# Sums of the first pair's operands made by GpSimd during the sequence stage and kept in DRAM

## The chip, the core and the metric

The kernel runs on one core of one Trainium2 chip. The metric is the device time of one execution in microseconds (us); lower is better. Five engines work side by side, each with an instruction queue that runs in order: TensorE (PE in the profile; its weight loads are PEld), VectorE (DVE), ScalarE (ACT), GpSimd (POOL) and SyncE (SP), which here only issues DMA transfers. ACT issues some transfers as well. An instruction that waits for a semaphore holds up everything behind it on its engine.

## The reference

Two branches work on x (2048 x 640, fp32) and are mixed by a gate for each row. Cut to what matters:

```python
g = sigmoid((x * gate_w).sum(-1, keepdims=True))
# A: Fourier mixing
a = einsum("bsd,ed->bse", x, dft_hid_re);  b = einsum("bsd,ed->bse", x, dft_hid_im)
y = einsum("ts,bse->bte", dft_seq_re, a) - einsum("ts,bse->bte", dft_seq_im, b)
# B: product-key experts, 32 heads, 16 x 16 keys, two best of 256 experts for each head
q = einsum("nd,dhc->nhc", x, w_q);  s1, s2 = scores of the halves of q with k1, k2
top_s, top_e = the two best sums of the two best of s1 and of s2
act = gelu(einsum("nd,nhkd->nhk", x, u[top_e]))
out = einsum("nhk,nhk,nhkd->nd", softmax(top_s), act, v[top_e])
return g * y + (1 - g) * out
```

## The kernel before

All large products are made in three fp32r matmuls (`mm3`, lines 127 to 129): each operand is split into a high half, a copy on ACT (line 122), and a low half, a subtraction on GpSimd or DVE (line 123).

**The sequence stage.** The sequence transform is done first, on x. It runs over 128 *pieces*, numbered n: w (real, imaginary) x c (four column blocks of 512 output rows) x s (16 blocks of x). For each piece SP loads a 128 x 512 tile `wf` of the DFT matrix five pieces ahead (`load_piece`, line 158), it is split three pieces ahead into the ring `WS` (`split_piece`; the low half on GpSimd), and PE makes 15 matmuls with it into five banks. After 16 pieces the five banks are copied to the staging tiles `ST` (line 212, ACT), gated by g on DVE (`gate_piece`, line 191) and stored to the DRAM tiles `pd[w, c]` (`store_piece`, line 198, ACT's queue). One such group is called a block q = 4w + c, and there are five `ST` tiles of 128 x 512, so a block is stored before the next is copied.

**What runs beside it.** From piece 31 to 70 the scores of branch B are made, then until the end of the stage the *experts*: DVE builds one-hot tiles `hot` (lines 539 to 541, three operations a tile, two tiles a set), PE multiplies them (line 563, 16 small matmuls a set, into a bank), and DVE sums the bank into `cd` (lines 547 and 549), which SP stores to the DRAM tile `gd` (line 553). Sets go in twos until the last pieces: six one-hot operations and four operations of sums a round. They are put between the matmuls by a pump with credits (`run_bg`), so their place on each engine is fixed when the program is written. Near the end of the stage DVE also makes sums of the hidden DFT matrices (`make_sums`, lines 648 to 652, tiles `tf` and `ts`), whose splits go to ACT, GpSimd and DVE.

**The last part.** The hidden transform is applied to what lies in `pd`, for two *pairs* b = 0 and 1 of column blocks, by a scheme with seven products in place of eight: `UNITS = ("a11", "a12", "s1", "s2", "s4", "s3", "a22")`. a11, a12, a21 and a22 are the blocks `pd[col - 1, 2 * b + row - 1]` (the first index of `pd` is real or imaginary), and s1, s2, s4 and s3 are sums of them: s1 = a22 + a21, s3 = a21 + a11, s2 = s1 + a11, s4 = s2 + a12. A unit has five steps k, 35 steps a pair. Step m multiplies the split operand (`step`); five steps ahead `split_step` splits it, out of raw tiles `ra` which `load_a` has loaded (line 705) and, for the s units, `add_a` has summed (line 708, DVE). In pair 0 and in pair 1 alike, the tile "s" holds s1, then s2, then s4: it is loaded with a22, and a21, a11 and a12 are added to it in turn, so that a11 and a12 are loaded twice. Raw tiles come from a free list of 19 (`take`, `give`). The experts' result enters by a product with v: `load_z` loads its parts, `split_z` multiplies them on DVE (lines 749 to 753) and splits them into `zo`, and `z_group` multiplies. At the end of a unit the banks are emptied by `post` (DVE and ACT) and, after a12, by a copy on ACT on line 860 into `ST[:, 4]`.

**What sets the order.** Every helper is hung on a place with `at(n, f, ...)`: it is called after piece n, or after step m as place 128 + m, in the order in which the `at` lines stand. Each engine's queue then runs its own instructions in that order.

## Time and profile before

| | |
|---|---|
| median of 3 runs | 794.71 us (794.21 to 794.85) |
| the profiled execution | 794.76 us, its span 793.0 us |
| PE busy | 778.2 us, 98% of the span, 4167 matmuls |
| DVE busy | 549.0 us, 69% |
| ACT, POOL busy | 275.1 us (35%), 338.7 us (43%) |
| mean granted TensorE clock | 0.996 |
| moved | 119.55 MB, 151 GB/s |

In the profile the engines stand by the names above; L123 is line 123 of the kernel before, and a name like `ra<-pd` is what an instruction writes and reads. Matmuls are pipelined, so that the recorded durations overlap: the pace of PE is read from start to start. An engine's idle time is told with what ended it.

### The profile page before, as it was taken

Reading aid. Unit: us, or ns where it says so; the run is one execution under the profiler, and the core shown is the slowest. Engines: PE = TensorE matmul, PEld = TensorE weight load, DVE = VectorE, ACT = ScalarE, POOL = GpSimd, SP = SyncE. Lnnn points to the kernel's source line nnn. Section 1 sums busy time; section 2 is a strip of 40 time slices with the busy share of each in tenths; the row PEclk is TensorE's granted clock in tenths of the full one; section 3 lists DMA queues with packets and bytes.
Section 4 is the critical chain, followed back from the end, with each engine's and each line's share of the span. In section 5 each row is a group of like instructions: output and inputs, shape, how many; then the busy total and the mean of one; then the engine's idle time right before and its main releaser. Section 6 shows DMA issues by size and latency. Waiting matters only on the chain.

```text
span 793.0 us, 10954 instructions
## 1 busy us (share of the span) xinstructions
PE 778.2 (98%) x4167; PEld 626.0 (79%) x4167; DVE 549.0 (69%) x658; ACT 275.1 (35%) x444; POOL 338.7 (43%) x234
## 2 busy tenths in 40 slices
PE   9999999999999999999999999999999997999997
PEld 6677677888888888888888888887887875888886
DVE  5851021286888799499969589989999938518651
ACT  3434223322315322532353551311333522534350
POOL 5432224315234241533415693334355453558270
PEclk9999999999999999999999999999999998999999
DMA  9876895503022330205213533235434586675321
GB/s 341 315 292 191 283 340 190 196 0 113 14 100 69 124 113 14 99 14 181 80 60 120 196 119 98 76 112 154 139 132 155 167 291 235 216 218 196 129 82 66
DMA packets 62787, 119.55 MB, mean 151 GB/s; under 512 B 8848, under 2 KB 15888, under 8 KB 62480
## 3 DMA queue, kind: packets, MB, share of 16 engines
q1 hardware_dynamic: 49984, 101.42, 38.3%
q10 hardware_dynamic: 12752, 17.45, 6.2%
q8 instruction: 32, 0.52, 0.3%
q14 instruction: 19, 0.16, 0.1%
HBM read 98.91 MB, written 19.93 MB: 150 GB/s over the span
## 4 chain that ended last, share of the span: by engine, by line
PE 90%; DVE 5%; DMA 3%; issue 1%; SPq 1%; ACT 0%; DVEq 0%; ACTq 0%
PE b L127 29%; PE b L129 28%; PE b L128 28%; PE b L299 2%; DMA xr<-in_xn 1%; PE b L563 1%; DMA wf<-in_wsre 1%; DMA ra<-pd 1%; PE b L311 1%; DVE tmp L547 0%; DVE hot L541 0%; DVE tf L651 0%; DVE tf L650 0%; DVE ST L191 0%; DVE ts L123 0%
## 5 line engine op out<-in xcount | busy, mean ns | idle before, releaser
L123 POOL TENSOR_TENSOR WS<-wf,WS 128x512 fp32r<-128x512 f32 x128 | 190.5, 1494 | 279.4 <-ACT WS L122 267.5
L127 PE MATMUL b<-WS,X 128*128 128x512 f32 x640 | 254.6, 398 | 1.2 <-ACT X L122 1.2
L129 PE MATMUL b<-WS,X 128*128 128x512 f32 x640 | 249.8, 390 | 0.5 <-DVE X L123 0.4
L128 PE MATMUL b<-WS,X 128*128 128x512 f32 x640 | 249.7, 390 | 0.3 <-POOL WS L123 0.3
L127 PEld LDWEIGHTS b<-WS,X 128*128 128x128 f32 x640 | 120.3, 188 | 34.6 <-issue 8.1
L129 PEld LDWEIGHTS b<-WS,X 128*128 128x128 f32 x640 | 120.1, 188 | 26.9 <-DVE X L123 1.3
L128 PEld LDWEIGHTS b<-WS,X 128*128 128x128 f32 x640 | 120.3, 188 | 24.2 <-POOL WS L123 0.7
L122 ACT ACTIVATE WS<-wf 128x512 fp32r<-128x512 f32 x128 | 80.2, 628 | 131.1 <-PE b L129 82.1
L413 DVE TENSOR_REDUCE mm<-sc 128x64 f32<-128x1024 f32 x32 | 39.0, 1219 | 45.0 <-ACT sc L399 44.5
L123 POOL TENSOR_TENSOR xl<-xf,xh 128x640 fp32r<-128x640 f32 x16 | 33.0, 2086 | 72.7 <-ACT xh L122 72.7
L127 PE MATMUL b<-WU,xh 128*128 128x512 f32 x160 | 62.7, 392 | 0.0
L129 PE MATMUL b<-WU,xl 128*128 128x512 f32 x160 | 62.3, 389 | 0.0
L128 PE MATMUL b<-WU,xh 128*128 128x512 f32 x160 | 62.3, 389 | 0.0
L399 ACT ACTIVATE sc<-b 128x512 f32<-128x512 f32 x32 | 20.5, 641 | 113.9 <-PE b L129 113.9
L123 POOL TENSOR_TENSOR WS<-ra,WS 128x512 fp32r<-128x512 f32 x32 | 45.2, 1434 | 28.5 <-ACT WS L122 28.5
L708 DVE TENSOR_TENSOR ra<-ra 128x512 f32<-128x512 f32 x40 | 37.6, 986 | 15.3 <-DMA ra<-pd 11.7
L314 DVE TENSOR_TENSOR WU<-b,WU 128x512 fp32r<-128x512 f32 (+1 forms) x16 | 7.8, 490 | 56.5 <-ACT WU L313 56.4
L415 DVE TENSOR_TENSOR eq<-sc,mm 128x1024 f16<-128x1024 f32 x32 | 45.5, 1423 | 1.1
L191 DVE SCALAR_TENSOR_TENSOR ST<-ST,grow 128x512 f32<-128x512 f32 x40 | 33.9, 910 | 16.7 <-DMA grow<-gdr 12.4
L123 POOL TENSOR_TENSOR WP<-ra,WP 128x512 fp32r<-128x512 f32 x18 | 28.5, 1588 | 30.1 <-ACT WP L122 23.6
L122 ACT ACTIVATE WS<-ra 128x512 fp32r<-128x512 f32 x46 | 28.5, 632 | 33.2 <-PE b L129 11.9
L419 DVE TENSOR_REDUCE rr<-eq 128x64 f16<-128x1024 f16 x32 | 39.0, 1220 | 1.1
(145 smaller groups left out, 1237.2 us busy)
## 6 DMA issues: line engine op xcount, KB each, us to landing
wq<-in_wq SPq DMA_DIRECT2D x32, 640.0 KB, 6.5
ra<-pd SPq DMA_DIRECT2D x70, 256.0 KB, 4.1
wf<-in_wsre SPq DMA_DIRECT2D x64, 256.0 KB, 5.6
wf<-in_wsim SPq DMA_DIRECT2D x64, 256.0 KB, 3.2
pd<-ST ACTq DMA_DIRECT2D x40, 256.0 KB, 2.8
xr<-in_xn SPq DMA_DIRECT2D x16, 320.0 KB, 6.0
xf<-in_xT SPq DMA_DIRECT2D x16, 320.0 KB, 3.3
out_y<-ST ACTq DMA_DIRECT2D x7, 512.0 KB, 3.4
```

What stands on the lines that cost most here:

```text
L122: nc.scalar.activation(h, f, AF.Copy)
L123: eng.tensor_sub(l, f, h.bitcast(F32))
L127: nc.tensor.matmul(o, wh, ah, start=first, stop=False, skip_group_check=more)
L128: nc.tensor.matmul(o, wh, al, start=False, stop=False, skip_group_check=more)
L129: nc.tensor.matmul(o, wl, ah, start=False, stop=last, skip_group_check=more)
L191: nc.vector.scalar_tensor_tensor(f, f, -1.0 if w else 1.0, g, op0=OP.mult, op1=OP.mult)
L299: nc.tensor.matmul(ps[32 * j:32 * j + 32, :HALF], kp[:, 8 * G // H, r, :], w[:, j], start=(r == 0), stop=(r == 1))
L399: nc.scalar.activation(scs[i].rearrange("p h e -> p (h e)")[:, c], ps, AF.Copy)
L413: nc.vector.tensor_reduce(m, sc, op=OP.max, axis=AX.X)
L415: nc.vector.tensor_tensor(eq, sc, m[:, :, None].to_broadcast([P, HH, E]), op=OP.is_equal)
L419: nc.vector.tensor_reduce(r, eq, op=OP.max, axis=AX.X)
L708: nc.vector.tensor_add(raw[b, o, k], raw[b, o, k], raw[b, what, k])
```

## The change

Five helpers are new. Behind piece 96, when block 5 (a22 of pair 0) lies gated in `ST`, `store_piece` keeps its five tiles as `P22` after they are stored. For each k, `load_parts` loads a21, a11 and a12 of pair 0 from `pd` into three tiles `ps`, `sum_parts` makes s1 and s3, then s2 and s4 in place by two times two additions on GpSimd, and `store_parts` stores the four to the new DRAM tiles `pq`. The places run from 95 (first load) to 111 (last stores). In the last part, pair 0 loads s1, s2, s4 and s3 from `pq`, each once, and has no additions; `load_z` of its first half moves from place 128 to 127; pair 1 is as before. The share of background work in the last part rises to 1.05 from step 6 on, not from step 10.

```diff
     pd = {(w, c): dram.tile([KD, P, TC], F32, name=f"pd{w}{c}", tag=f"pd{w}{c}") for w in range(2) for c in range(NC)}
+    pq = {u: dram.tile([KD, P, TC], F32, name=f"pq{u}", tag=f"pq{u}") for u in ("s1", "s2", "s4", "s3")}
...
     def store_piece(q):
         w, c = divmod(q, NC)
+        if q == NC + 1:
+            P22.update((d, staged[q, d]) for d in range(KD))
...
     def load_a(b, what, k, row, col):
-        nc.sync.dma_start(take((b, what, k)), pd[col - 1, 2 * b + row - 1][k])
+        f = take((b, what, k))
+        nc.sync.dma_start(f, pd[col - 1, 2 * b + row - 1][k] if row else pq[what][k])
...
+    PS, parts = [], {}
+
+    def load_parts(k):
+
+        if not PS:
+            PS.extend(big.tile([P, 2, TC], F32, name="ps", tag=t) for t in ("xf", "xh", "xl"))
+        parts[k] = [t[:, k % 2] for t in PS]
+        for f, q in zip(parts[k], ((0, 1), (0, 0), (1, 0))):
+            nc.sync.dma_start(f, pd[q][k])
+
+    def sum_parts(k, n):
+        f21, f11, f12 = parts[k]
+        f22 = P22[k]
+        if n == 0:
+            nc.gpsimd.tensor_add(f22, f22, f21)
+            nc.gpsimd.tensor_add(f21, f21, f11)
+        else:
+            nc.gpsimd.tensor_add(f11, f11, f22)
+            nc.gpsimd.tensor_add(f12, f12, f11)
+
+    def store_parts(k, n):
+        f21, f11, f12 = parts[k]
+        for u, f in (("s2", f11), ("s4", f12)) if n else (("s1", P22[k]), ("s3", f21)):
+            nc.sync.dma_start(pq[u][k], f)
+
+    for k, (n, m) in enumerate(((-1, 2), (0, 4), (5, 7), (7, 9), (10, 12))):
+        n, m = NT * (NC + 2) + n, NT * (NC + 2) + m
+        at(n, load_parts, k)
+        for a in range(2):
+            at(m + a, sum_parts, k, a)
+            at(m + 2 + a, store_parts, k, a)
...
-            if what in ("a11", "a12", "a22", "s3", "s4"):
+            if b == 0 or what in ("a11", "a12", "a22", "s3", "s4"):
                 give(key)
...
+    M = NPC
+    for k in range(KD):
+        at(M - 6 + k, load_a, 0, "a11", k, 1, 1)
+        at(M - 4 + min(k, 3), load_a, 0, "a12", k, 1, 2)
+        at(M + k // 2, load_a, 0, "s1", k, 0, 0)
+        at(M + 2 + k, load_a, 0, "s2", k, 0, 0)
+        at(M + 7 + k, load_a, 0, "s4", k, 0, 0)
+        at(M + 12 + k, load_a, 0, "s3", k, 0, 0)
+        at(M + 18 + k, load_a, 0, "a22", k, 2, 2)
...
-        share = 1.05 if m >= 10 else 0.0
+        share = 1.05 if m >= 6 else 0.0
```

GpSimd's queue from piece 101's split on, before and then now (`x32` are 32 such operations in a row; the last 32 of `WS<-wf` ahead of the splits of `ts` are the splits of the pieces 87 to 118):

```order
L123 TENSOR_TENSOR DD<-draw,DD 128x640
L123 TENSOR_TENSOR WS<-wf,WS 128x512 x32
L123 TENSOR_TENSOR ts<-tf,ts 128x256 x2
L123 TENSOR_TENSOR WS<-wf,WS 128x512 x2
L123 TENSOR_TENSOR ts<-tf,ts 128x256 x2
```

```order
L123 TENSOR_TENSOR WS<-wf,WS 128x512 x15
L732 TENSOR_TENSOR ST<-ST,ps 128x512
L733 TENSOR_TENSOR ps<-ps 128x512
L123 TENSOR_TENSOR WS<-wf,WS 128x512
L735 TENSOR_TENSOR ps<-ps,ST 128x512
L736 TENSOR_TENSOR ps<-ps 128x512
L123 TENSOR_TENSOR WS<-wf,WS 128x512
L732 TENSOR_TENSOR ST<-ST,ps 128x512
L733 TENSOR_TENSOR ps<-ps 128x512
L123 TENSOR_TENSOR WS<-wf,WS 128x512
```

Two additions now stand behind each split, from that of piece 101 to that of piece 112, with none behind those of 105 and 110; the splits that follow stand behind them.

SP's queue from the load of the gate's row at place 94 on, before and then now (`pqs` are the DRAM tiles of the sums, numbered; `gd<-cd` is the store of the experts' sums of pair 0):

```order
L158 DMA wf<-in_wsim 128x512 x9
L553 DMA gd<-cd 16x4x2048 x2
L158 DMA wf<-in_wsim 128x512 x7
L184 DMA grow<-gdr 128x512
L158 DMA wf<-in_wsim 128x512
```

```order
L159 DMA wf<-in_wsim 128x512
L556 DMA gd<-cd 16x4x2048 x2
L741 DMA pqs_78<-ps 128x512
L741 DMA pqs_79<-ps 128x512
L726 DMA ps<-pd_70 128x512
L726 DMA ps<-pd_69 128x512
L726 DMA ps<-pd_73 128x512
L159 DMA wf<-in_wsim 128x512 x2
L741 DMA pqs_77<-ST 128x512
L741 DMA pqs_80<-ps 128x512
```

The piece of now begins at the load of piece 108: between the store of gd and the next load of wf, that of piece 109, now stand two stores and three loads; before, the load of wf followed at once.

DVE's queue at the start of the last part, from the gating of the last block on, before and then now:

```order
L191 SCALAR_TENSOR_TENSOR ST<-ST,grow 128x512 x5
L708 TENSOR_TENSOR ra<-ra 128x512
L749 TENSOR_SCALAR ra<-ra 128x512
L752 TENSOR_TENSOR ra<-ra 128x512
L753 TENSOR_TENSOR ra<-ra 128x512
L752 TENSOR_TENSOR ra<-ra 128x512
L753 TENSOR_TENSOR ra<-ra 128x512
L708 TENSOR_TENSOR ra<-ra 128x512 x8
L123 TENSOR_TENSOR WS<-ra,WS 128x512
```

```order
L192 SCALAR_TENSOR_TENSOR ST<-ST,grow 128x512 x5
L786 TENSOR_SCALAR ra<-ra 128x512
L789 TENSOR_TENSOR ra<-ra 128x512
L790 TENSOR_TENSOR ra<-ra 128x512
L789 TENSOR_TENSOR ra<-ra 128x512
L790 TENSOR_TENSOR ra<-ra 128x512
L123 TENSOR_TENSOR WS<-ra,WS 128x512
```

The additions are gone; the operations on the experts' parts come right behind the gating, and the first split of an s operand right behind them.

More of the change, by code (lines that the diff above doesn't have):

```diff
@@ L179, in gated_mix_kernel @@
     p3, last_part, ending, share = None, False, False, 0.95
-    grow, staged = {}, {}
+    grow, staged, P22 = {}, {}, {}
     def load_row(q):
@@ L719, in split_step @@
             what = UNITS[u]
-            key = (b, "s" if what in ("s1", "s2", "s4") else what, k)
+            key = (b, "s" if b and what in ("s1", "s2", "s4") else what, k)
             sp[m] = ring(m)[:, 0], ring(m)[:, 1]
@@ L881, in quarter @@
         at(NPC + b * NSTEP + 6 * KD, post, b, "q")
+    M = NPC
[7 more added lines that the diff above has]
+        at(M + 18 + k, load_a, 0, "a22", k, 2, 2)
+    M = NPC + NSTEP
+    for k in range(KD):
+        at(M - 8 + k, load_a, 1, "a11", k, 1, 1)
+        at(M - 4 + k, load_a, 1, "a12", k, 1, 2)
+        at(M + k, load_a, 1, "s", k, 2, 2)
+        at(M + k, load_a, 1, "s3", k, 2, 1)
+        at(M + 4 + k, add_a, 1, "s", "s3", k, False)
+        at(M + 5 + k, load_a, 1, "a11", k, 1, 1)
+        at(M + 8 + k, add_a, 1, "s", "a11", k, False)
+        at(M + 8 + k, add_a, 1, "s3", "a11", k, True)
+        at(M + 8 + k, load_a, 1, "a12", k, 1, 2)
+        at(M + 13 + k, add_a, 1, "s", "a12", k, True)
+        at(M + 21 + k, load_a, 1, "a22", k, 2, 2)
     for b in range(2):
         M = NPC + b * NSTEP
-        for k in range(KD):
-            at(M - (8 if b else 6) + k, load_a, b, "a11", k, 1, 1)
-            at(M - 4 + min(k, 4 if b else 3), load_a, b, "a12", k, 1, 2)
-            at(M + k, load_a, b, "s", k, 2, 2)
-            at(M + k, load_a, b, "s3", k, 2, 1)
-            at(M + 4 + k, add_a, b, "s", "s3", k, False)
-            at(M + 5 + k, load_a, b, "a11", k, 1, 1)
-            at(M + 8 + k, add_a, b, "s", "a11", k, False)
-            at(M + 8 + k, add_a, b, "s3", "a11", k, True)
-            at(M + 8 + k, load_a, b, "a12", k, 1, 2)
-            at(M + 13 + k, add_a, b, "s", "a12", k, True)
-            at(M + 21 + k, load_a, b, "a22", k, 2, 2)
-        for n, i in ((0, -1 if b else 0), (1, 21)):
+        for n, i in ((0, -1), (1, 21)):
             at(M + i, load_z, b, n)
```

## The prediction

> **What bounds the kernel now.** I read the page first, then the list of PE's waits, then PE's own timeline, then the chain, and at the end the two engines that the change loads. The page:

> ```profile
> PE 778.2 (98%) x4167; PEld 626.0 (79%) x4167; DVE 549.0 (69%) x658; ACT 275.1 (35%) x444; POOL 338.7 (43%) x234
> DVE  5851021286888799499969589989999938518651
> ```

> PE is busy for 98% of the span, so only PE's idle time and slow clock can be won, and any new wait of PE is lost in full. DVE has 69% on average but eights and nines in slices 23 to 31 (counted from 0, 19.8 us each, 456 to 634 us): there it is nearly full. That is where the change puts its new work. PE waits three times for more than a moment after the start:

> ```profile
> PE b L127 <- ACT ST L860: 5.0, 1, 5.0
> PE b L563 <- DVE tmp L547: 1.3, 1, 1.3
> PE b L128 <- POOL zo L123: 1.2, 2, 0.9
> ```

> PE's timeline puts numbers to them (start, duration, and in brackets the idle time before):

> ```profile
> 609.76 0.44 PE L563 MATMUL b<-hot 128*64 128x64 f16 x16 [1.33 <-DVE tmp L547]
> 626.61 0.44 PE L563 MATMUL b<-hot 128*64 128x64 f16 x16
> ...
> 649.55 0.39 PE L127 MATMUL b<-zo,vxh 128*128 128x512 f32 x1
> 650.25 0.50 PE L128 MATMUL b<-zo,vxh 128*128 128x512 f32 x1 [0.31 <-POOL zo L123]
> 652.20 0.49 PE L127 MATMUL b<-zo,vxh 128*128 128x512 f32 x1
> 653.54 0.50 PE L128 MATMUL b<-zo,vxh 128*128 128x512 f32 x1 [0.85 <-POOL zo L123]
> 655.52 0.39 PE L127 MATMUL b<-WS,ts 128*128 128x512 f32 x1
> 655.75 0.40 PE L128 MATMUL b<-WS,ts 128*128 128x512 f32 x1
> 656.66 0.39 PE L129 MATMUL b<-WS,ts 128*128 128x512 f32 x1
> 662.07 0.80 PE L127 MATMUL b<-WS,DD 128*128 128x512 f32 x1 [5.01 <-ACT ST L860]
> ...
> 668.07 0.40 PE L129 MATMUL b<-WP,ts 128*128 128x512 f32 x1
> ```

> The pace is read from start to start: 655.52 to 656.66 are five matmuls, 0.228 each. The big hole is at 656.66: the next matmul starts 5.41 later, 5.18 more than the pace. And after it PE is slow: from 662.07 to 668.07 stand 14 matmuls in 6.00 us, where the pace needs 14 x 0.228 = 3.19. The hole thus costs 5.18 + 2.81 = 8.0. The two waits for zo cost 0.70 - 0.23 and 1.34 - 0.23, together 1.58. The chain says what stands behind them:

> ```profile
> 570.55 0.70 DVE tmp L547
> ...
> 609.11 0.61 DVE tmp L547
> ...
> 651.69 5.44 DMA ra<-pd
> ...
> 659.04 1.75 DVE ra L708
> 661.43 0.59 ACT ST L860
> 662.07 0.80 PE b L127
> ```

> At 662 it is the sums of pair 0: a late load, DVE's addition on L708, then the split on ACT that waits for it, and behind that split in ACT's queue the copy L860 that empties PE's bank. From 570.55 to 609.76 the chain runs through DVE alone: PE's 1.33 there says that DVE has no slack left at 609.76. What DVE loses ahead of that, beyond its idle time, PE loses too.

> **Part one: the last part.** Removed are the 20 additions on DVE of pair 0, in this row of the operations on the tiles ra between 640 and 680 (least, median and most ns, first and last start); the 35 loads of pair 0 stay 35.

> ```profile
> L708 DVE TENSOR_TENSOR ra<-ra x20: 677/684/1791, 644.5 to 675.0; 128x512 f32<-128x512 f32 x20
> ```

> With s1 loaded ready-made the split of step 10 waits for no addition, and ACT reaches L860 on time: 8.0 back, the whole hole with its slow stretch. The load of the expert operand moves ahead of the s loads, one place earlier, so I count the 1.58 too. Gain 9.6. DVE's time for 20 additions is not a gain by itself, since PE waits for it only in that hole. The least would be 8.0 (zo as late as before), and none if the s1 loads land late (a rival below). The bank of L860 needs nothing else that the change touches.

> The slow clock is a row, 2.81 of the 9.6. [...]

> The share of background work that starts at step 6 and not at 10 costs nothing: the last of the 512 expert matmuls stand at 626.61, ahead of the last part, and nothing is left to pump.

> **Part two: behind piece 96.** Added are 15 loads, 20 additions on GpSimd, 20 stores, all between the places 95 and 111. The stores and loads go through SP's queue, the additions stand in POOL's between the low halves of the wf pieces (L123), which PE needs. No DVE instruction is added there, but POOL and DVE hold each other up. These are DVE's rows, first in a stretch where POOL always had work, then one in which it had little, and POOL's rows beside them:

> ```profile
> 459.92 1.77 DVE L541 TENSOR_TENSOR hot<-hot,rows 128x1024 f16<-128x1024 f16 x1
> 461.62 2.07 DVE L539 TENSOR_TENSOR hot<-rows,wtab 128x1024 f16<-128x1024 f16 x1
> ...
> 528.89 0.69 DVE L547 TENSOR_TENSOR tmp<-b,mask 128x512 f32<-128x512 f32 x1 [0.70 <-PE b L563]
> 531.73 0.68 DVE L539 TENSOR_TENSOR hot<-rows,wtab 128x1024 f16<-128x1024 f16 x1
> 532.33 1.78 DVE L540 TENSOR_TENSOR hot<-rows,wtab 128x1024 f16<-128x1024 f16 x1
> 534.03 0.68 DVE L541 TENSOR_TENSOR hot<-hot,rows 128x1024 f16<-128x1024 f16 x1
> ```

> ```profile
> 459.41 1.74 POOL L123 TENSOR_TENSOR WS<-wf,WS 128x512 fp32r<-128x512 f32 x1
> ...
> 518.91 2.95 POOL L123 TENSOR_TENSOR WS<-wf,WS 128x512 fp32r<-128x512 f32 x2 [3.61 <-ACT WS L122]
> ...
> 558.52 1.71 POOL L123 TENSOR_TENSOR WS<-wf,WS 128x512 fp32r<-128x512 f32 x1 [2.93 <-ACT WS L122]
> ...
> 587.23 2.54 POOL L123 TENSOR_TENSOR WS<-wf,WS 128x512 fp32r<-128x512 f32 x2 [1.09 <-ACT WS L122]
> ```

> A one-hot operation of DVE alone takes 0.60 from start to start (531.73 to 532.33); with a 128x512 POOL operation beside it 1.70 (459.92 to 461.62, 532.33 to 534.03). So one POOL operation that meets the one-hot phase costs DVE 1.10, and under a queue of them the two take turns. The four operations of a sums phase (L547, L549) start at 528.89 and end at 531.73, 2.84, whatever POOL does; there POOL runs undisturbed at 2.54 / 2 = 1.27. The splits of the pieces 101 and 112, behind which the first and the last additions stand, are those at 518.91 and 558.52. The stretch of the change, and DVE's longest wait in it:

> ```profile
> core 0: us, PE busy (x) PEld busy (x) DVE busy (x) ACT busy (x) POOL busy (x), PEclk, DMA share, GB/s
> 520.50:570.50 50.00, 50.00 (x402) 40.20 (x396) 46.58 (x60) 11.10 (x18) 18.91 (x15) 1.00 0.41 127
> 570.50:609.70 39.20, 37.93 (x254) 30.73 (x247) 38.42 (x57) 12.99 (x30) 21.86 (x18) 1.00 0.44 151
> ```

> ```profile
> DVE tmp L547 <- PE b L563: 2.7, 4, 1.1
> ```

> 60 DVE operations are six rounds of six one-hots and four sums: 6 x (3.6 + 2.84) = 38.6 without POOL. Busy are 46.6, so 15 POOL operations cost 8.0, which is 7.3 hits of 1.10, about one for every second. Idle are 3.4, most of it waits for PE. With 20 additions POOL has 35 operations in the stretch. Queued as they are, two or three behind each split, they fill the sums phases, 6 x 2.84 / 1.27 = 13.4 of them, and the other 21.6 meet one-hots, of which there are 36: 23.7 us. DVE then needs 38.6 + 23.7 = 62.3 for work that must be done in 50.0 if PE is not to wait: 12.3 too much, with all its idle time used up. Bounds: at the rate of before (0.48 hits each) 35 cost 18.7 and DVE is 7.3 late; if all 20 additions hit, 30.0 and 18.6 late. If none does, nothing. I take 12.3, since the row of 459 to 462, POOL with a queue, is nearest to what the new order makes. From 570.5 to 609.7 DVE is busy for 38.4 of 39.2, so nothing of the 12.3 is worked off before PE's wait at 609.76. PE may stop earlier too, at an L563 whose bank the sums of the group before still read; that is part of the 12.3 and not added to it.

> [...]

> The queues. On SP the new loads and stores stand among the loads of wf:

> ```profile
> 540.48 1.26 SPq L553 DMA_DIRECT2D gd<-cd  x2
> 542.15 10.89 SPq L158 DMA_DIRECT2D wf<-in_wsim  x7
> ```

> and from the list of transfers between 629 and 661, the median time to landing at its end:

> ```profile
> ra<-pd SPq DMA_DIRECT2D x22, 256.0 KB, 5.2
> ```

> The store of gd waits for DVE's sums; it will be some 8 us later. Behind it stand two stores, three loads that overwrite what they read, and only then the wf of piece 109. I estimate 549 for gd, one landing of 5.2 for the stores, another for the loads and wf: about 561, and the split of piece 109 behind two additions near 565. The split of piece 112 was at 558.52, so that of 109 would come later than 112's did before, and some 3 to 5 us of PE's loss may show there. It runs beside the DVE debt of 12.3 and is hidden by it; if that debt is smaller, this is what remains. The 35 transfers themselves (9 MB in 60 us) have room at a DMA share of 0.41. ACT gets nothing new. Its copies into ST at place 111 wait for the last store of s1; that is due some us ahead.

> **The sum.** The profiled execution took 794.76, 0.05 over the median of 794.71. 794.76 - 9.6 + 12.3 = 797.5.

> **Rivals.** First, faster: POOL, not DVE, does the waiting, or the additions fall mostly into the sums phases. For it: seven hits for 15 operations says that about half slip through, and the loads space the additions. Against it: two or three in a row cannot all fit in 2.84. It decides the sign at a DVE debt of 9.6, which is (50.0 + 9.6 - 38.6) / 1.10 = 19 hits of 35. With 5 of the 20 hitting, 12.3 hits, the debt is 2.1: 787.3; with none 785.2.

> Second, the additions hit at the rate of before, 7.3 late: 792.5, and with a little queueing 793 to 796, no change that can be told.

> Third, slower by more: s1 lands late and L860's wait stays. For it: a load between 629 and 661 takes 5.2 to land, and the expert loads now stand ahead of s1. Against it: five loads feed step 10 now, where ten and five more did, and the first matmul on s1 is due at 655.52 less the 1.58 of zo, near 653.9. Then the 8.0 stay lost: 805.5.

> **Chances.** The forecast's case (debt 11 to 18.6, 796.3 to 804) 0.46; the third rival 0.09; the second 0.22, of which 0.15 within 0.2% (about 1.6 us, what a measurement of this kernel tells from no change) and 0.07 under it; the first 0.23. That is 0.55 slower, 0.15 the same, 0.30 faster. The range of 788 to 804 leaves out the best of the first rival and the third, under 0.2 in all; the likeliest case alone has 796.3 to 804.

> **What would show it.** In the profile after, one-hot operations between 520 and 585 should mostly take 1.7 in place of 0.6, PE should wait for tmp (L547 before) by 10 to 14 us in total up to piece 123, and in pair 0 there should be no wait for ST and no stretch at 0.43 a matmul. It is wrong if DVE still idles in that stretch, if the additions stretch and DVE's operations do not, or if PE waits in pair 0 for another load.

## The result and the profile after

The changed kernel takes 808.54 us (808.06 to 809.5, 4 runs), the one before 794.46 (793.62 to 794.85, 4 runs) on the same chip. The ratio is 1.0182, with a 95% interval of 1.0167 to 1.0197: slower by 14.1 us. The profiled execution took 808.06, its span is 806.3.

In the kernel after, the lines behind 131 have moved: the one-hots are L542 to L544, the sums L550 and L552, the experts' matmul L566, the copies into `ST` L215, the additions on GpSimd L732 to L736, the operations on the experts' parts L786 to L790. The page of the kernel after, busy time of the engines and DVE's slices:

```profile
PE 781.8 (97%) x4167; PEld 627.7 (78%) x4167; DVE 549.5 (68%) x638; ACT 273.3 (34%) x444; POOL 369.7 (46%) x254
DVE  4841021386887899599788599999999942417651
```

DVE has 20 instructions fewer and is busy for as long as before (549.5 against 549.0). Its nines now stand without a gap in slices 23 to 31, where two eights stood before; the part of the last slices, where the additions were, is emptier. PE has the same 4167 matmuls in the same order, so each can be set beside itself in the kernel before. PE's waits after the start:

```profile
PE b L566 <- DVE tmp L550: 8.9, 4, 4.9
PE b L128 <- POOL WS L123: 4.4, 4, 1.6
PE b L127 <- ACT WS L122: 3.2, 1, 3.2
PE b L127 <- ACT ST L215: 1.5, 1, 1.5
```

The wait of 5.0 for the copy L860 and those for zo are gone, and four kinds stand in their place. PE's timeline of the kernel after says where:

```profile
547.04 0.44 PE L566 MATMUL b<-hot 128*64 128x64 f16 x16 [1.83 <-DVE tmp L550]
548.55 0.44 PE L566 MATMUL b<-hot 128*64 128x64 f16 x16 [1.07 <-DVE tmp L550]
...
563.98 0.50 PE L128 MATMUL b<-WS,X 128*128 128x512 f32 x1 [1.16 <-POOL WS L123]
568.29 0.50 PE L128 MATMUL b<-WS,X 128*128 128x512 f32 x1 [0.61 <-POOL WS L123]
...
624.97 0.64 PE L566 MATMUL b<-hot 128*64 128x64 f16 x16 [4.85 <-DVE tmp L550]
...
626.13 0.63 PE L128 MATMUL b<-WS,X 128*128 128x512 f32 x1
626.56 0.63 PE L129 MATMUL b<-WS,X 128*128 128x512 f32 x1
...
667.48 0.51 PE L127 MATMUL b<-WS,DD 128*128 128x512 f32 x1 [3.21 <-ACT WS L122]
669.53 0.79 PE L128 MATMUL b<-WS,DD 128*128 128x512 f32 x1 [1.55 <-POOL WS L123]
```

The matmul at 624.97 is the one that stood at 609.76 before. So the account of the change, by how late a matmul is against its own time before:

| place | late by (us) | what was added there |
|---|---|---|
| up to 537 us | +0.1 | |
| 624.97, the last long wait for DVE | +15.2 | waits for the experts' sums, for three pieces and for one bank, and 3.4 us at 0.43 a matmul behind the wait at 548.55 |
| 628.7 | +16.6 | 1.4, PE at 0.43 a matmul after that wait |
| 667 to 673, last step of a12 in pair 0 | +23.3 | 6.7, a wait for splits that is new, and a slow stretch behind it |
| end of pair 0 on | +13.4 | 9.9 won: no waits for zo, no hole at the copy |

794.76 + 16.6 + 6.7 - 9.9 = 808.2; the profiled execution took 808.06.

**The stretch of the change.** DVE's sums rounds (first L547 or L550 of each) began at 520.6, 528.9, 537.5, 545.7, 554.4, 562.2 and 570.6 before. After, the same seven began at 520.6, 533.5, 546.3, 553.6, 564.4, 577.2 and 586.6. DVE's timeline of the kernel after shows the one-hots of such a round, and POOL's what stands beside them:

```profile
523.47 1.63 DVE L542 TENSOR_TENSOR hot<-rows,wtab 128x1024 f16<-128x1024 f16 x1
525.02 1.77 DVE L543 TENSOR_TENSOR hot<-rows,wtab 128x1024 f16<-128x1024 f16 x1
526.71 1.78 DVE L544 TENSOR_TENSOR hot<-hot,rows 128x1024 f16<-128x1024 f16 x1
```

```profile
524.51 1.73 POOL L735 TENSOR_TENSOR ps<-ps,ST 128x512 f32<-128x512 f32 x1
526.32 1.62 POOL L736 TENSOR_TENSOR ps<-ps 128x512 f32<-128x512 f32 x1
527.91 1.72 POOL L123 TENSOR_TENSOR WS<-wf,WS 128x512 fp32r<-128x512 f32 x1
```

From start to start the one-hots take 1.55 to 1.7, and POOL's operations start within them one by one. The stretch as a whole, and DVE's longest wait in it:

```profile
core 0: us, PE busy (x) PEld busy (x) DVE busy (x) ACT busy (x) POOL busy (x), PEclk, DMA share, GB/s
520.50:587.10 66.60, 60.46 (x444) 47.66 (x437) 64.31 (x61) 11.18 (x19) 53.87 (x36) 0.97 0.60 198
587.10:624.90 37.80, 30.82 (x206) 24.51 (x205) 36.72 (x57) 12.05 (x29) 19.53 (x16) 0.95 0.51 175
```

```profile
DVE cd L552 <- DMA gd<-cd: 1.2, 1, 1.2
```

Six rounds now take 66.6 in place of 50.0, and DVE is busy for 64.3 of them. Without POOL the rounds need 38.6, so 25.7 are hits, 23.4 of 1.10; in the timeline 25 of the 36 one-hots take 1.4 or more. Idle remain 2.3, the 1.2 for a store of `gd` and else short gaps between operations; the prediction had counted all of it as used up. Up to PE's long wait DVE works 1.4 of it off.

**The new wait in the last part.** ACT's timeline of the kernel after (its first two rows are for the copies into `ST`, judged below), and then the chain of waits:

```profile
576.28 0.63 ACT L122 ACTIVATE WS<-wf 128x512 fp32r<-128x512 f32 x1 [2.35 <-DMA wf<-in_wsim]
576.82 2.53 ACT L215 ACTIVATE ST<-b 128x512 f32<-128x512 f32 x5
...
654.87 0.62 ACT L122 ACTIVATE WS<-ra 128x512 fp32r<-128x512 f32 x1
662.99 0.63 ACT L122 ACTIVATE zo<-ra 128x512 fp32r<-128x512 f32 x1 [7.50 <-DVE ra L790]
666.28 0.63 ACT L122 ACTIVATE zo<-ra 128x512 fp32r<-128x512 f32 x1 [2.66 <-DVE ra L790]
666.81 1.14 ACT L122 ACTIVATE WS<-ra 128x512 fp32r<-128x512 f32 x2
```

```profile
659.42 1.90 DMA ra<-gd
661.54 0.70 DVE ra L789
...
668.22 1.27 POOL WS L123
```

The two splits into zo wait on ACT for DVE, which waits for the experts' load (the row `ra<-gd`). In the kernel before, ACT's rows at this place were:

```profile
641.43 0.63 ACT L122 ACTIVATE WS<-ra 128x512 fp32r<-128x512 f32 x1 [1.41 <-DMA ra<-pd]
648.21 0.63 ACT L122 ACTIVATE zo<-ra 128x512 fp32r<-128x512 f32 x1 [6.14 <-DVE ra L753]
651.51 0.63 ACT L122 ACTIVATE zo<-ra 128x512 fp32r<-128x512 f32 x1 [2.67 <-DVE ra L753]
```

There two splits `WS<-ra` in a row stood ahead of them in ACT's queue (the second is the row at 641.43) and one behind; now one stands ahead and two behind. The one that changed sides is the split for step 9, which PE needs before zo. `split_z` stands four places behind `load_z` in the code, and so it moved with it, from place 132 to 131. At 666.81 the split comes at last, POOL's half at 668.22, and PE has waited 3.21 and 1.55 and run at half pace behind it.

### The profile page after: what moved, and what is told of

It reads as the page before. It is cut to its first block, busy times and chain, and to the rows that moved or that the text cites. A ratio compares the mean times of both kernels' runs of the same rounds, so it can differ in the third digit from the quotient of the medians.

```text
span 806.3 us, 11032 instructions
## 1 busy us (share of the span) xinstructions
PE 781.8 (97%) x4167; PEld 627.7 (78%) x4167; DVE 549.5 (68%) x638; ACT 273.3 (34%) x444; POOL 369.7 (46%) x254
## 4 chain that ended last, share of the span: by engine, by line
PE 80%; DVE 13%; DMA 4%; issue 1%; SPq 1%; POOL 0%; ACT 0%; DVEq 0%; ACTq 0%; POOLq 0%
PE b L127 26%; PE b L129 25%; PE b L128 25%; PE b L302 2%; DVE hot L544 2%; DVE hot L543 2%; DVE hot L542 2%; DVE tmp L550 1%; DVE cd L552 1%; DMA xr<-in_xn 1%; DVE ST L192 1%; DMA pd<-ST 1%; DMA wf<-in_wsre 1%; DMA gd<-cd 1%; PE b L566 1%
## 5 line engine op out<-in xcount | busy, mean ns | idle before, releaser
L123 POOL TENSOR_TENSOR WS<-wf,WS 128x512 fp32r<-128x512 f32 x128 | 193.7, 1521 | 253.0 <-ACT WS L122 244.3
L127 PE MATMUL b<-WS,X 128*128 128x512 f32 x640 | 256.3, 400 | 2.7 <-ACT ST L215 1.5
L128 PE MATMUL b<-WS,X 128*128 128x512 f32 x640 | 251.4, 393 | 2.8 <-POOL WS L123 2.8
L129 PE MATMUL b<-WS,X 128*128 128x512 f32 x640 | 250.8, 392 | 0.1
L127 PEld LDWEIGHTS b<-WS,X 128*128 128x128 f32 x640 | 120.9, 189 | 36.7 <-issue 7.5
L128 PEld LDWEIGHTS b<-WS,X 128*128 128x128 f32 x640 | 121.1, 189 | 28.3 <-POOL WS L123 4.8
L129 PEld LDWEIGHTS b<-WS,X 128*128 128x128 f32 x640 | 121.0, 189 | 26.9 <-DVE X L123 1.0
L122 ACT ACTIVATE WS<-wf 128x512 fp32r<-128x512 f32 x128 | 80.0, 628 | 144.6 <-PE b L129 58.3
L123 POOL TENSOR_TENSOR xl<-xf,xh 128x640 fp32r<-128x640 f32 x16 | 33.1, 2086 | 73.1 <-ACT xh L122 73.1
L127 PE MATMUL b<-WU,xh 128*128 128x512 f32 x160 | 62.7, 392 | 0.0
L129 PE MATMUL b<-WU,xl 128*128 128x512 f32 x160 | 62.3, 389 | 0.0
L128 PE MATMUL b<-WU,xh 128*128 128x512 f32 x160 | 62.3, 389 | 0.0
L123 POOL TENSOR_TENSOR WS<-ra,WS 128x512 fp32r<-128x512 f32 x32 | 43.4, 1377 | 29.4 <-ACT WS L122 29.2
L418 DVE TENSOR_TENSOR eq<-sc,mm 128x1024 f16<-128x1024 f32 x32 | 45.5, 1423 | 1.1
L123 POOL TENSOR_TENSOR WP<-ra,WP 128x512 fp32r<-128x512 f32 x18 | 27.6, 1541 | 30.0 <-ACT WP L122 29.8
L544 DVE TENSOR_TENSOR hot<-hot,rows 128x1024 f16<-128x1024 f16 x32 | 39.8, 1244 | 0.0
L543 DVE TENSOR_TENSOR hot<-rows,wtab 128x1024 f16<-128x1024 f16 x32 | 39.6, 1237 | 0.0
## 6 DMA issues: line engine op xcount, KB each, us to landing
wf<-in_wsre SPq DMA_DIRECT2D x64, 256.0 KB, 5.6
wf<-in_wsim SPq DMA_DIRECT2D x64, 256.0 KB, 4.1
ra<-pd SPq DMA_DIRECT2D x50, 256.0 KB, 3.2
pd<-ST ACTq DMA_DIRECT2D x40, 256.0 KB, 2.9
ra<-pqs SPq DMA_DIRECT2D x20, 256.0 KB, 4.8
```

Of the source, the lines that this page charges most:

```text
L122: nc.scalar.activation(h, f, AF.Copy)
L123: eng.tensor_sub(l, f, h.bitcast(F32))
L127: nc.tensor.matmul(o, wh, ah, start=first, stop=False, skip_group_check=more)
L128: nc.tensor.matmul(o, wh, al, start=False, stop=False, skip_group_check=more)
L129: nc.tensor.matmul(o, wl, ah, start=False, stop=last, skip_group_check=more)
L418: nc.vector.tensor_tensor(eq, sc, m[:, :, None].to_broadcast([P, HH, E]), op=OP.is_equal)
```

## Experiments

All are told by their ratio to the kernel before, run on the same chip beside them, with its 95% interval.

**e1: the split of zo back in its old place.** The changed kernel with one number altered:

```diff
-            at(M + i + 4, split_z, b, n)
+            at(M + i + (5 if b == n == 0 else 4), split_z, b, n)
```

> The changed kernel with the splits of pair 0's expert operand one place later again (place 132 instead of 131), the loads still early. Theory A (order on ACT): the changed kernel lost 6.6 us at step 9 because the split of step 9 stands in ACT's queue behind the two zo splits, which wait for the expert loads; with the order of before the 6.6 go: 808.5 - 6.6 = 802, up to 803.5 if PE then waits for zo as before (1.6). Theory B (late transfers: step 9's own operand or the loads around it land late): the wait stays, 807 to 809.

Measured: 802.33 us (801.26 to 802.81), ratio 1.0099 [1.0084, 1.0114], 6.2 below the changed kernel. ACT's timeline of this kernel:

```profile
655.29 1.31 ACT L122 ACTIVATE WS<-ra 128x512 fp32r<-128x512 f32 x2
661.82 0.63 ACT L122 ACTIVATE zo<-ra 128x512 fp32r<-128x512 f32 x1 [5.22 <-DVE ra L790]
```

and PE's waits:

```profile
PE b L566 <- DVE tmp L550: 9.8, 5, 4.9
PE b L128 <- POOL WS L123: 2.5, 3, 1.1
```

Both splits are done before zo is waited for, and PE has no wait for ACT's `WS` left. PE is 16.5 late at the start of the last part and 6.6 at its end: 9.9 comes back, the waits for zo among it, with `split_z` where it stood before (`load_z` stays at 127). The order cost 6.2 us, and the earlier `split_z` won nothing. The edit moves the operations of `split_z` on DVE and GpSimd as well; that it was ACT's queue that held the split is read from the row at 666.81, which follows the one for zo without idle time.

**e2 and e3: the additions and the transfers apart.** e2 leaves the 20 additions out and keeps the loads and stores; e3 keeps the additions and leaves out the 20 stores and nine of the 15 loads, so that six of the 35 transfers stay. (It also lets pair 0 load unsummed blocks from `pd`, a line of the edit that is not shown.)

```diff
 # e2
-            at(m + a, sum_parts, k, a)
 # e3
-        for f, q in zip(parts[k], ((0, 1), (0, 0), (1, 0))):
+        for f, q in zip(parts[k], ((0, 1), (0, 0), (1, 0)) if k < 2 else ()):
...
-            at(m + 2 + a, store_parts, k, a)
```

> The changed kernel without the 20 additions on GpSimd; all loads and stores stay, so the s operands hold unsummed blocks. Theory A (GpSimd's additions hold up DVE's one-hots): PE's delay of 16.6 us up to piece 127 falls to 0 to 2, one-hots are back at 0.6 between GpSimd's splits, and the time is 808.5 - 16 = 791 to 794, with the wait at step 9 still there. Theory B (the 35 transfers and SP's queue make the delay): it stays at 10 or more and the time over 802.

> The changed kernel with the 20 additions, but without the stores to DRAM and with six of the 15 loads (the additions work on what lies in the tiles; pair 0 then loads unsummed blocks in place of the sums). Theory A: the additions alone make the delay, 13 to 17 us up to piece 127, 805 to 809. Theory B (transfers): under 4 us, 793 to 797. If both share, between.

Measured: e2 794.53 (791.58 to 795.87, 10 runs), ratio 0.9998 [0.9985, 1.0011]; e3 805.98 (805.22 to 806.33), ratio 1.0145 [1.013, 1.016]. The stretch of e2, then that of e3:

```profile
520.50:570.50 50.00, 50.00 (x393) 40.21 (x394) 45.45 (x59) 10.88 (x19) 19.18 (x15) 1.00 0.68 227
```

```profile
520.50:587.10 66.60, 59.88 (x432) 48.06 (x427) 65.32 (x64) 11.74 (x19) 53.39 (x36) 0.92 0.33 100
```

In e2 all 35 transfers run (DMA share 0.68, before 0.41), though the stores no longer wait for additions, and PE loses nothing up to the wait at 609.76 (it is 0.4 late from the start of the run, and stays so); DVE is busy for 45.5 of 50.0, as before. In e3 most transfers are gone (0.33), DVE is as busy as after, and PE comes 14.8 late into the last part, where after it is 16.6. So the additions make the debt. The transfers alone cost PE nothing there; beside the additions they add 2.6 us to the whole (808.54 - 805.98). e2 still ends level with the kernel before: the waits below cost it 2.5 at 609.76 and 6.7 at step 9, their slow stretches included, and that takes all of the 9.2 that it wins behind them.

```profile
PE b L127 <- ACT WS L122: 3.1, 1, 3.1
PE b L566 <- DVE tmp L550: 2.2, 1, 2.2
```

**e4: both.** e2 and e1 in one kernel, so that neither cost is there and the gain stands alone.

> Both together: no additions on GpSimd, and the zo splits one place later (the s operands hold unsummed blocks). Theory A: only the gain of the last part is left, 9.6 us at most and 8 at least: 785 to 787. Theory B (some further loss in the transfers or the last part): 789 or more.

Measured: 786.55 (784.87 to 787.51), ratio 0.99 [0.9882, 0.9917]. PE's one wait for the experts' sums:

```profile
PE b L566 <- DVE tmp L550: 1.8, 1, 1.8
```

It is 7.8 below the kernel before with which it was timed (794.37). In the profile 9.9 are won in the last part and 2.1 lost at this one wait and the slow stretch behind it. The four kernels also give each cost twice. The split's place costs 6.2 with the additions (808.54 - 802.33) and 8.0 without (794.53 - 786.55); the additions cost 14.0 with the early split and 15.8 with the late one.

**e7: the same additions on DVE.** e1 with the 20 additions moved to the other engine:

```diff
-            nc.gpsimd.tensor_add(f22, f22, f21)
+            nc.vector.tensor_add(f22, f22, f21)
```

and likewise the other three.

> The changed kernel with zo splits one place later and the 20 additions on DVE in place of GpSimd, at the same places. Theory A (an addition on GpSimd costs DVE 1.1 whenever it meets a one-hot, one on DVE 0.6): 20 x 0.6 = 12.0 and up to 3 us of new meetings with GpSimd's splits, less 3.4 of idle time: 786.5 + 9 to 12 = 795 to 798, faster than the 802.3 on GpSimd. Theory B (what costs is the queueing behind loads and stores, whatever engine adds): 801 to 804 or more.

Measured: 798.35 (797.76 to 800.28), ratio 1.0052 [1.0036, 1.0068], just over what the expectation had and 4.0 below e1. Its stretch of six rounds and DVE's rows in it:

```profile
520.50:584.20 63.70, 55.72 (x401) 44.59 (x401) 60.79 (x80) 10.85 (x18) 20.27 (x14) 0.95 0.64 209
```

```profile
527.23 0.68 DVE L735 TENSOR_TENSOR ps<-ps,ST 128x512 f32<-128x512 f32 x1
527.94 1.65 DVE L736 TENSOR_TENSOR ps<-ps 128x512 f32<-128x512 f32 x1
```

An addition takes DVE 0.7, or 1.6 (527.94). With the additions on GpSimd DVE was busy for 64.3 in six rounds, with them on DVE itself for 60.8, and before for 46.6: 0.89 and 0.71 for each addition. Giving this work to the other engine cost DVE more time than doing it; the two ratios agree, 1.0099 against 1.0052 with intervals apart.

**e5, e6 and e8: only s1 made ahead.** The hole in the kernel before hung on s1 alone. e5 makes only s1 ahead (5 loads of a21, 5 additions on DVE, 5 stores), sums s2, s4 and s3 in the last part as before, and keeps `split_z` late:

```diff
+    def load_part(k):
...
+        nc.sync.dma_start(parts[k], pd[0, 1][k])
+    def sum_part(k):
+        nc.vector.tensor_add(parts[k], P22[k], parts[k])
+    def store_part(k):
+        nc.sync.dma_start(pq["s1"][k], parts[k])
+    for k in range(KD):
+        n = NT * (NC + 2)
+        at(n - 1, load_part, k)
+        at(n + 2 + k, sum_part, k)
+        at(n + 4 + k, store_part, k)
...
+        at(M + k // 2, load_a, 0, "s", k, 0, 0)
+        at(M + 4 + k, load_a, 0, "s3", k, 2, 1)
```

e6 has `nc.gpsimd` in `sum_part`. e8 is e5 with a21 for s3 loaded nine places later and its addition moved from place M + 8 + k to M + 17 + k; the second loads of a11 stand one place earlier.

> Only s1 of pair 0 is made ahead, by five additions on DVE behind the pieces 98 to 102 (five loads, five stores); s2, s4 and s3 are summed in the last part as before, but a21 is loaded after s1; zo splits one place later. Five additions of 0.6 are 3.0 us of DVE, which idles 3.4 there. Theory A (the hole at step 10 is the late operands of s1 alone, and DVE time up to its idle time is free): PE's delay up to piece 127 under 2, the hole with its slow clock gone, 786 to 788, level with the 786.5 of the kernel without additions. Theory B (the other sums of the last part make a new wait): 789 to 794.

> The same with the five additions on GpSimd. At 0.48 hits of 1.1 they cost DVE 2.6 us, at one hit each 5.5, against 3.4 of idle time: 0 to 2 us of delay, 786 to 789. If GpSimd's additions cost as in the changed kernel (16.6 us for 20, or 0.83 each) without using idle time: 4.2 us more than the kernel without additions, 790.7.

> As the kernel with s1 made ahead on DVE, but the loads of a21 for s3 and their sums stand behind those of s2 and s4 (places 141 to 149, sums at 145 to 149) and the second loads of a11 one place earlier. Theory A: what was left there (PE's wait for a low half at the fourth step of s4 with the slow pace behind it, 2.9 us) came from the loads and additions for s3 ahead of those for s2 and s4; it goes: 789.8 - 2.9 = 787, and up to 1 less. Theory B (the chain of additions s, s2, s4 on DVE with the splits behind it on ACT is what is late): it stays within 1 of 789.8.

| | us | range | ratio to before | 95% interval |
|---|---|---|---|---|
| e5 | 789.79 | 789.27 to 791.13 | 0.9942 | 0.9929 to 0.9955 |
| e6 | 791.18 | 790.38 to 792.89 | 0.9962 | 0.9947 to 0.9977 |
| e8 | 789.11 | 786.69 to 789.68 | 0.9929 | 0.9913 to 0.9946 |

All three are faster than the kernel before and than the changed one. Between e5 and e6 the intervals touch, so the engine of five additions is not settled by them. e5 came out as theory B of its expectation has it, a new wait in the last part; e6 0.5 above the dearer of its two estimates; e8 within 1 of e5, its theory B. PE's waits in e5:

```profile
PE b L566 <- DVE tmp L550: 2.1, 1, 2.1
PE b L128 <- POOL WS L123: 1.4, 1, 1.4
```

The second is in the units on s4, where each step still waits for its chain of additions. e8 was to free it, and did not: by the matmuls' own times PE loses 2.6 there in place of 2.7, and the times of the kernels can't be told apart. What holds s4 is thus not s3's load and addition. The trace of e5 has two candidates, and neither was tried. The first low half for s4 on GpSimd starts 1.5 ahead of PE's first matmul on s4 (671.11 and 672.66), where before it was 5.8 ahead (674.74 and 680.58), which speaks for the chain from s1 over s2 to s4 being late. And four of these low halves take 7.97 in place of 5.73, with DVE at work beside them, which speaks for hits.

## Why the prediction was wrong

The sign was right. The time was 11 us too low, outside the range of 788 to 804. By the prediction's own steps, in the profiled execution (808.06 against 797.5), the account is:

- **"ACT gets nothing new"** is the step that failed, and it held 6.7 of the 10.6 us that were missed; without it (e1) the time is 802.33, inside the range. Nothing new is issued on ACT, but two instructions that wait moved ahead of one that PE needs. The prediction followed the order on SP, POOL and DVE, where instructions were added, and not on ACT, where only `split_z` shifted by a place. The 1.58 of zo, which it put down to that earlier place, came in e1 as well, with the split in its old one. None of the rivals had this wait.
- **The DVE debt, 12.3.** The mechanism held: at the matmul of 609.76 PE is 1.3 late without the additions (e2, 0.4 of it from the start), 13.2 with them and few transfers (e3) and 15.2 with all. The size was 2.9 short, 15.2 at PE's wait. Hits were 23.4 where 21.6 were counted (2.0 us), and 2.3 of DVE's idle time were not used, 1.2 of it a wait for a store of `gd`, the rest short gaps; 1.4 was then worked off by 624.9, where the prediction had nothing. The upper bound, 18.6, held.
- **No slow clock behind the debt.** 2.81 were counted as won where a wait ends, but nothing as lost where a new one is made. Behind the wait at 624.97 it is 1.4. (The one behind 548.55 lies ahead of that wait, and is hidden by it.)
- **The gain, 9.6,** measured 9.9: 8.0 for the hole and its slow stretch, as counted, and 1.9 for zo.
- **SP's queue.** Estimated were 549 for the store of gd, 561 for the piece behind the additions and 565 for its split; gd was issued at 549.25 and PE waited for the splits at 563.98 and 568.29. That this loss is hidden by the debt held for the most part: e3, with six of the 35 transfers, is 1.8 less late (14.8 against 16.6), and whether that is these two waits or the transfers' other effects was not told apart. That ACT's copies into `ST` would find their tiles free also held: PE's 1.5 for L215 follows a piece of wf that landed late (2.35 at 576.28), not a store. It was close: in e1 one of these copies waited 0.85 for a store of s1. That the higher share from step 6 on costs nothing was not tried by itself; the last of the experts' matmuls stands at 643.20, ahead of the last part, as the prediction argued.
- **The rivals.** The debt decided the sign at 9.6, and it was above. The first and second rival, with fewer hits, are not what came. The third, a late s1, did not come either: neither the copy nor `ST` is waited for in pair 0. It came nearest in height (805.5), by a wait that was not there, which is luck.
- **The signs.** The one-hots at 1.7 came. PE's waits for the experts' sums add up to 8.9, below the 10 to 14 that were named, because waits for pieces and a bank took part of the debt. The sign against it, a wait in pair 0 for another load, came too: step 9 stands behind the experts' load, with 3.4 us at 0.43 a matmul behind it.

So the sum with what was measured in each place is 797.5 + 6.7 + 2.9 + 1.4 - 0.3 = 808.2.

## What to carry to other kernels

When a step is moved on an in-order queue, list for every engine, also one that gets no new work, which instruction now stands behind a waiting one and who needs it; one place of a split that waits for a load cost 6 to 8 us here. Before work is handed from DVE to GpSimd, compare what the other engine's operation takes from DVE (0.89 here) with what DVE itself takes for it (0.71). And make ahead only the part that the critical wait hangs on: with five additions of the twenty the kernel was 4.9 us faster, of the 7.8 that are there when the additions are left out.

## What the runs showed of the hardware

A slow stretch followed a wait of PE of 2.05 us in e5 and none a wait of 2.99 in e6, so here its length alone did not decide. In e5, PE's timeline:

```profile
610.17 0.44 PE L566 MATMUL b<-hot 128*64 128x64 f16 x16 [2.05 <-DVE tmp L550]
...
611.01 0.63 PE L128 MATMUL b<-WS,X 128*128 128x512 f32 x1
...
614.00 0.45 PE L129 MATMUL b<-WS,X 128*128 128x512 f32 x1
```

From 611.01 to 614.00 stand seven matmuls at 0.43, 0.20 more each than the pace, 1.4 in all. The kernel before had waited 1.33 at the same place (its row at 609.76 stands in the prediction) and ran on at 0.24 (from 610.47 to 610.71). So e5, with a wait that is 0.7 longer, lost about 2 us. But e6 waited longer still, and no slow stretch followed:

```profile
611.70 0.44 PE L566 MATMUL b<-hot 128*64 128x64 f16 x16 [2.99 <-DVE tmp L550]
```

The granted clock (PEclk, the third figure from the end in the rows by stretch) shows the difference. In the profiles of the kernels before and after it changes only at whole multiples of 3.41 us from its first rise (at 5.71 and 6.92): up to the last matmul at 661.07 and 667.90 before, and at 549.64, 553.05, 621.32, 628.14, 669.10 and 672.52 after. Cut into steps on such a grid, the wait and what follows it are, for e5 and then for e6:

```profile
607.30:610.71 3.41, 1.36 (x35) 0.88 (x35) 3.38 (x6) 1.97 (x5) 1.88 (x3) 1.00 0.89 330
610.71:614.12 3.41, 3.41 (x9) 2.65 (x10) 3.38 (x7) 0.63 (x1) 2.38 (x2) 0.50 0.05 16
```

```profile
606.72:610.13 3.41, 1.99 (x24) 1.36 (x23) 3.31 (x5) 0.95 (x3) 3.41 (x4) 1.00 1.01 318
610.13:613.55 3.42, 1.85 (x22) 1.56 (x22) 3.38 (x5) 1.86 (x5) 1.73 (x2) 1.00 0.49 184
```

The step of e5 at 0.50, in which PE is busy throughout, was followed by the full pace: 0.23 a matmul from 614.53 to 614.76.

One operation of GpSimd and one one-hot of DVE held each other up, in turns: the one-hot went from 0.60 (from 531.73 to 532.33, before) to 1.70 (from 459.92 to 461.62, before), GpSimd's operation from 1.27 (two in the 2.54 at 587.23, before) to 1.73 (at 524.51, after). With GpSimd busy for 53.9 of 66.6 us, where it had been for 18.9 of 50.0, that raised DVE's need for six rounds from 46.6 to 64.3.
